# A delta rule with a routed expert layer: later index stores for the middle router run, and 816 rows an expert

## The chip, the core and the metric

The kernel runs on one core of a Trainium2 chip. A core has a matrix engine (TensorE, PE in the profile; its weight loads are shown as PEld), a vector engine (VectorE, DVE), a scalar engine (ScalarE, ACT), a general engine (GpSimd, POOL) and an engine that issues transfers (SyncE, SP). Each takes its own instructions in order, and they wait for one another by semaphores. Transfers run on 16 DMA engines; SP, ACT and POOL issue them. The metric is the time of one execution on the device in microseconds (us).

## The reference, cut to what matters

Two blocks follow one another. The first is a delta rule: for 4 batches and 8 heads of width 48 a state of 48 x 48 is carried over 768 steps.

```python
for t in range(S):
    y[:, :, t] = np.einsum('bhd,bhde->bhe', q[:, :, t], state)
    v_old = np.einsum('bhde,bhd->bhe', state, kt)
    state = state + bt[:, :, :, None] * np.einsum('bhd,bhe->bhde', kt, vt - v_old)
```

Its 3072 tokens of width 384 are then routed to the two best of eight experts by noisy logits, and each expert is a layer of 384 to 1024 to 384:

```python
noisy_logits = x @ w_gate + np.log1p(np.exp(x @ w_noise)) * noise
top2 = np.argpartition(-noisy_logits, 2, axis=1)[:, :2]
# top2_w: the two logits' softmax
for e in range(E):
    for k in range(2):
        mask = top2[:, k] == e
        h = np.maximum(x[mask] @ w1[e], 0.0)
        out[mask] += top2_w[mask, k, None] * (h @ w2[e])
```

## The kernel before

**Two stages.** `deltanet` (from L463) computes the delta rule, the routing and a first part of expert 0; after it, a loop over experts 1 to 7 does the rest. All is in 32-bit floating point.

**The delta rule.** The 768 steps are cut into 12 chunks of 64; two chunks make a step `s`, of which there are NS = 6, with US = 4 units each (a unit is one chunk of two batches). A unit ends in `answer`: a last product on PE (L1012), a copy by ACT to a buffer `y` of a ring of four (L1038), a store of it to memory by SP (L399, `rows_y`), three transposes on PE (L1022) and the product with the router's weights (L1027).

**The router.** `route(g)` runs three times, by `ROUTES = [(0, 3), (3, 2), (5, 1)]`: for steps 0 to 2, for steps 3 and 4 (the middle run), and for step 5. DVE finds for each token its two experts, and the row that the token gets in each expert's list: the `slot`s (the last of them are written at L1157). Then POOL stores for each unit, once for each of the two choices, a record (token, weight, place) at those rows of `tokens_x` in memory, with an indirect DMA of 128 records (L441, `spread`). These are the index stores: 24 for the first run, 16 for the middle one, 8 for the last.

**The early part of expert 0.** After step 2 and after step 4 (`EARLY`) enough of expert 0's tokens are known to start on them. `early_rows(s)` has SP read the table of the first records (`early_meta`, L1282) and POOL gather the rows that it names (`early_x`, L405): two blocks of 128 rows in the first group, three in the second. `early(s, lo, hi)` then transposes them on PE (L1326), multiplies by w1 (L1347, results rectified by ACT at L1358) and by w2 (L1371), in three batches: blocks 0 and 1, blocks 2 and 3, block 4.

**What sets the order.** Inside `deltanet` nothing is issued directly. Each piece is added to a list (`jobs.add`) with its engine, an estimated cost, the names that it reads and writes, and perhaps a due time (`due`), a spacing (`apart`), or a latest class (`late`). `Jobs.order` carries the due times backwards along the dependences and then walks forward through an estimated time, taking on each engine the most urgent job that could start. The result is the order in which each engine's instructions are issued; SP and POOL, which issue transfers, are ordered in the same way. What an instruction waits for on the chip is decided separately, from the buffers that it really touches and from the dependences that are added by hand: a name in `reads` alone places a job in the order, and makes no semaphore.

A name in the list `looked_up` of `route` makes a run's stores come behind the reads of the early tables of earlier steps. In POOL's queue the end of the delta rule stands thus, behind the last scaling of v (L917): the last of the first run's stores, two gathers of the first early group, the sixteen stores of the middle run, the three gathers of the second group, the eight stores of the last run. SP has, at the same place, the first table read, the stores of the last two `y`, the second table read (which waits for all stores of steps 0 to 4) and the loads of expert 1's weights.

**The experts.** An expert takes ROWS = TILES * 128 + MORE rows = 832 of its list. Should one have more tokens, a fallback after the loop (`tc.If(count > ROWS)`) does the remaining ones. `load_metas` reads the lists (L425, after every index store), `load_rows` gathers six blocks of 128 rows and one of MORE into `xr` (L405), `regroup` moves them by DMA into `xq` (L1609), and `turns` transposes these on DVE into `xe` (L1619). The first product is a fast scheme with 20 block products instead of 24, in which an operand has half the rows, RH = ROWS / 2 = 416 columns (`first`, by `PLAN`; all of its matmuls are issued at L1595, and its sums of operands at L1561). ACT copies and rectifies (L1651, L1662), DVE adds (L1656). The second product (`second`, also L1595, 192 columns) and the last rows (`last_rows`, L1706: MORE rows, in two halves of the array side by side) follow, and POOL adds the gated rows to the output (L460). `rest` does for expert 0 the 192 rows that the early part left (L1735 to L1768), while POOL and DVE prepare expert 1.

The lines of the hand-over are these; the rest stands below.

```python
turn_r = turn_of[s][0]
if s + 1 == sum(ROUTES[turn_r]):
    route(turn_r)
if s in EARLY:
    cut(s, EARLY[s][-1][1] * 128)
    early_rows(s)
```

Of the kernel before, what the change touches and what calls it, by code (L numbers as in the profile page):

```python
# [21 lines left out]
Q = 32  # L22
QS = 128 // Q
TILES = 6
MORE = 64
# [212 lines left out]
def kernel(  # L238
# [231 lines left out]
    def deltanet(ictx):  # L470
# [611 lines left out]
        def route(g):  # L1082
# [141 lines left out]
            for x in range(units):  # L1224
                of, i = first_s + x // US, x % US
                for y, to in enumerate(slot):
                    jobs.add(
                        POOL, 1.3,
                        lambda x=x, of=of, y=y, to=to: [
                            spread(metas(g)[:, x, y], to[:, x : x + 1], of, columns)  # L1230
                        ],
                        reads=[("slot", g % 2), meta, ("num", g % 2), "blank", *looked_up],
                        writes=[("rows", of, i, y)], lands=2.0, moves=0.2,
                        due=FIRST + (s + paced) * PACE + BEHIND + jobs.AFTER,
                        apart=jobs.APART * paced,
                    )

# [36 lines left out]
        def early_rows(s):  # L1274
# [6 lines left out]
            def load_meta():  # L1281
# [9 lines left out]
                SP, 0.7, load_meta, reads=of_steps, lands=2.0, moves=0.3, due=FIRST + s * PACE + BEHIND,  # L1291
# [3 lines left out]
            for at in range(lo, upto):  # L1295
                x, x_key = early_x[at], ("early_x", at)
                jobs.add(
                    POOL, 1.2,
                    lambda x=x, at=at: [take_rows(x, place_of(early_meta[:, at]), units)],
                    reads=[("early_meta", lo), *(("stored", i) for i in range(units))],  # L1300
                    writes=[x_key], lands=2.0, moves=0.7, due=FIRST + s * PACE + BEHIND,
                )
# [130 lines left out]
        for s in range(NS):  # L1433
# [37 lines left out]
            turn_r = turn_of[s][0]  # L1471
            if s + 1 == sum(ROUTES[turn_r]):
                route(turn_r)
            if s in EARLY:
                cut(s, EARLY[s][-1][1] * 128)
                early_rows(s)
# [26 lines left out]
    with ExitStack() as ectx:  # L1503
# [96 lines left out]
        def load_rows(e):  # L1600
            for i, size in enumerate(rows_in):
                take_rows(xr[0:size, i], place_of(metas_x[0:size, e, i]), NT)
# [13 lines left out]
        def turns():  # L1616
# [4 lines left out]
            some = TILES // 2  # L1621
            for i in range(2):
# [7 lines left out]
            more = MORE // Q  # L1630
            yield turn(
                xe[:, :, MAIN : MAIN + MORE].rearrange("p k (g x) -> p k g x", g=more),
                xq[:, 0:more, TILES].rearrange("p g (j k) -> p k g j", k=KT),
            )
# [295 lines left out]
```

## Time and profile before

| what | value |
|---|---|
| timed runs | 813.46, 810.22, 808.51 us; median 810.22 |
| the profiled execution | 825.89 us |
| its span, first to last instruction | 824.1 us |
| PE busy | 718.1 us, 87% of the span |
| PEld busy | 561.7 us |
| DVE busy | 541.7 us |
| POOL busy | 417.7 us |
| ACT busy | 307.8 us |
| mean granted clock of PE | 0.887 |
| DMA traffic | 79.60 MB |

The profile is one execution taken by the hardware profiler. Its page gives for each engine the busy time and its course in 40 slices of about 20.6 us (a digit is tenths of the slice), the clock that PE was granted in tenths of full speed (PEclk), groups of instructions by source line with their number and mean time, and what ended the idle time before them. Answers of the trace list the instructions of one engine in order of time (start, length, engine, line, operation, tiles out<-in, shape, number, and in brackets the idle time before with its cause), or the busy time of all engines in given stretches. "issue" stands for idle time for which the profile shows no cause. Ends of matmuls are modelled, so their starts are the safer marks.

The delta rule takes the first 323 us or so, the early part of expert 0 goes from there to 383 us, `rest` to 401 us, and the experts 1 to 7 take 58.6 us each.

### The profile page before, as it was taken

How to read it: one execution, taken by the hardware profiler on the slowest of the kernel's cores; microseconds unless marked ns; L12 is line 12 of the kernel's file. 1: busy time of each engine (PE TensorE's matmuls, PEld its weight loads, DVE VectorE, ACT ScalarE, POOL GpSimd, SP SyncE). 2: the span in 40 equal slices, each digit the busy share in tenths (PEclk: the TensorE clock that was granted, in tenths of full speed). 3: DMA queues.
4: the chain of work that ended last, by engine and by line, in shares of the span. 5: the costliest groups of instructions: out<-in, count | busy, mean ns of one | idle time of the engine just before them, and what ended most of it. 6: DMA issues, size and time to landing. Idle time of an engine off the chain costs nothing.

```text
span 824.1 us, 22389 instructions
## 1 busy us (share of the span) xinstructions
PE 718.1 (87%) x9319; PEld 561.7 (68%) x9319; DVE 541.7 (66%) x1100; ACT 307.8 (37%) x728; POOL 417.7 (51%) x408
## 2 busy tenths in 40 slices
PE   5656888887788862999999999999999999999993
PEld 3445777776677752778568668678588597596693
DVE  7899969898762420303488488587686785785831
ACT  3758486856445421122250340430520511502500
POOL 5030021021133445459678777786886886787032
PEclk8556788888677685999999999999999999999997
DMA  3457544322434011335644535544544446333031
GB/s 68 88 103 179 139 127 105 81 61 62 127 71 119 3 52 59 134 84 85 181 114 117 124 102 121 136 132 72 151 145 93 107 138 130 89 58 41 2 39 24
DMA packets 142719, 79.60 MB, mean 97 GB/s; under 512 B 118352, under 2 KB 139024, under 8 KB 141584
## 3 DMA queue, kind: packets, MB, share of 16 engines
q1 hardware_dynamic: 125840, 57.25, 26.8%
q0 software_dynamic: 12800, 19.80, 13.3%
q8 instruction: 75, 1.23, 0.7%
q10 hardware_dynamic: 3968, 1.03, 0.6%
q14 instruction: 36, 0.29, 0.1%
HBM read 49.85 MB, written 20.03 MB: 85 GB/s over the span
## 4 chain that ended last, share of the span: by engine, by line
PE 62%; DVE 14%; issue 12%; POOL 4%; ACT 2%; SPq 2%; DMA 1%; another core or an unknown queue 0%; DVEq 0%; POOLq 0%
PE inner L1595 24%; PE outer L1595 12%; DVE w2e L766 4%; PE pair L1347 3%; PE pair L635 3%; PE pair L1371 3%; DVE w1e L770 2%; POOL out_dram L460 2%; PE single L1027 2%; PE pair L1012 2%; PE inner L1706 2%; PE pair L975 2%; PE single L619 2%; DVE w2e L770 1%; PE pair L953 1%
## 5 line engine op out<-in xcount | busy, mean ns | idle before, releaser
L1662 ACT ACTIVATE hT<-inner 128x416 f32<-128x416 f32 x112 | 57.9, 517 | 260.9 <-PE inner L1595 257.6
L1656 DVE TENSOR_TENSOR hT<-hT,inner 128x416 f32<-128x416 f32 x182 | 105.5, 587 | 63.5 <-PE inner L1595 55.3
L460 POOL DMA_INDIRECT out_dram<-sums,metas_x x51 | 83.4, 1635 | 94.7 <-DVE sums L1495 67.3
L441 POOL DMA_INDIRECT tokens_x<-meta,slot x48 | 47.5, 989 | 79.6 <-DVE w2e L770 22.0
L1595 PE MATMUL inner<-s_x,w1e 128*128 128x416 f32 x196 | 78.7, 512 | 0.0
L917 POOL TENSOR_TENSOR v<-v,norms 128x384 f32<-128x384 f32 x24 | 23.7, 1008 | 91.1 <-DMA rows_y<-y 44.6
L405 POOL DMA_INDIRECT xr<-rows_y,metas_x x49 | 55.8, 1138 | 19.6 <-issue 12.8
L1651 ACT ACTIVATE hT<-hT 128x416 f32<-128x416 f32 x112 | 59.9, 547 | 12.1 <-DVE hT L1656 6.5
L1595 PEld LDWEIGHTS inner<-s_x,w1e 128*128 128x128 f32 x196 | 37.2, 190 | 31.2 <-issue 28.8
L1595 PE MATMUL inner<-xe,w1e 128*128 128x416 f32 x140 | 58.1, 513 | 0.0
L1595 PE MATMUL outer<-t_w,hT 128*128 128x192 f32 x336 | 58.0, 326 | 0.0
L1595 PE MATMUL inner<-s_x,s_w 128*128 128x416 f32 x140 | 56.9, 512 | 0.0
L1595 PEld LDWEIGHTS outer<-t_w,hT 128*128 128x128 f32 x336 | 55.2, 190 | 0.0
L1561 POOL TENSOR_TENSOR w1e<-w1e 128x256 f32<-128x256 f32 x63 | 52.8, 846 | 2.3
L1595 PE MATMUL outer<-w2e,hT 128*128 128x192 f32 x280 | 50.7, 328 | 0.3
L1595 PEld LDWEIGHTS outer<-w2e,hT 128*128 128x128 f32 x280 | 46.1, 190 | 4.3 <-issue 2.1
L1595 PEld LDWEIGHTS inner<-s_x,s_w 128*128 128x128 f32 x140 | 26.6, 190 | 22.3 <-issue 22.3
L824 ACT COPY w<-tt_tb 32x256 f32<-32x256 f32 x96 | 38.6, 402 | 6.8 <-DVE tt_tb L801 4.2
L1595 PE MATMUL outer<-t_w,s_h 128*128 128x192 f32 x224 | 40.6, 329 | 0.0
L1595 PEld LDWEIGHTS inner<-xe,w1e 128*128 128x128 f32 x140 | 26.4, 190 | 20.7 <-issue 16.5
L1491 DVE TENSOR_SCALAR sums<-outer,metas_x 128x192 f32<-128x192 f32 x70 | 27.8, 411 | 18.2 <-PE outer L1595 17.5
L1595 PEld LDWEIGHTS outer<-t_w,s_h 128*128 128x128 f32 x224 | 36.6, 190 | 4.2 <-issue 4.2
(202 smaller groups left out, 1586.7 us busy)
## 6 DMA issues: line engine op xcount, KB each, us to landing
w1e<-in_moe_w_dram SPq DMA_DIRECT2D x8, 1536.0 KB
w2e<-in_moe_w_dram SPq DMA_DIRECT2D x8, 1536.0 KB
v<-in_v_dram SPq DMA_DIRECT2D x48, 96.0 KB
qp<-in_q_dram SPq DMA_DIRECT2D x48, 96.0 KB
out_dram<-empty SPq DMA_DIRECT2D x4, 1152.0 KB
rows_y<-y SPq DMA_DIRECT2D x24, 192.0 KB
xq<-xr SPq DMA_DIRECT2D x52, 84.0 KB
kp<-in_k_dram SPq DMA_DIRECT2D x88, 48.0 KB
```

Of the source, the lines that this page charges most:

```text
L405: d = nc.gpsimd.indirect_dma_start(out=got, out_offset=None, in_=rows_y[0 : units * 128], in_offset=bass.IndirectOffsetOnAxis(ap=index, ax ...
L441: d = nc.gpsimd.indirect_dma_start(out=tokens_x, out_offset=bass.IndirectOffsetOnAxis(ap=slot, axis=0), in_=meta, in_offset=None, bounds_c ...
L460: d = nc.gpsimd.indirect_dma_start(out=out, out_offset=bass.IndirectOffsetOnAxis(ap=index, axis=0), in_=got, in_offset=None, bounds_check= ...
L635: nc.tensor.matmul(out[to(z, b), z, j], kT[rows_of[z], j, crossed(z, b)], rhs(z, j, b), start=(j == 0), stop=(j == NP - 1), skip_group_che ...
L766: v_.tensor_tensor(out=part, in0=t[:, :, j + 1 :, j, None].to_broadcast(shape), in1=t[:, :, None, j, 0:j].to_broadcast(shape), op=ALU.mult,)
L824: lambda rows=rows, cols=cols, w64=w64, tt=tt: nc.scalar.copy(w64[rows, :, cols], tt[rows]),
L1491: nc.vector.tensor_scalar_mul(got, p, gate)
L1561: engine.tensor_tensor(out=block(to), in0=block(x), in1=block(y), op=ALU.add if sign == "+" else ALU.subtract,)
L1595: nc.tensor.matmul(p, lhsT, rhs, start=opens and i == 0, stop=i == len(products) - 1, skip_group_check=True,)
L1651: nc.scalar.activation(h, h, ACTF.Relu)
L1656: nc.vector.tensor_tensor(out=h, in0=h, in1=p, op=ALU.add if sign > 0 else ALU.subtract)
L1662: nc.scalar.mul(h, p, float(sign))
```

## The change

There are three parts in the diff.

The index stores of the middle router run (`s + 2 == NS`, so steps 3 and 4) are no longer added to the list right after its slots. `route` now returns a function that adds them, `spread_all`; for the middle run it is held back and called after the last step's answers have been added. There the stores read one more name, the `y` of the last unit, their due time is one step later, and they lose their spacing. The other two runs call it at once, without that name.

The second early group's table read and gathers (`early_rows` for step 4) are added there too, behind those stores, and come due two steps later.

An expert takes 816 rows instead of 832: MORE is 48. The gather of the last block (`load_rows`), its regrouping and its transpose keep the depth of 64 rows, now named TAKEN. Since 64 rows of that transpose reach into the columns of the next part of `xe`, it moves from the end of `turns` to its start, and the later transposes overwrite the surplus. Everything that is made from ROWS, RH or MORE follows: 408 columns in the first product, 176 columns in `rest`, 48 rows in the last blocks.

```diff
@@ -22,7 +22,7 @@
 Q = 32
 QS = 128 // Q
 TILES = 6
-MORE = 64
+MORE, TAKEN = 48, 64
 EARLY_BANK = 2, (0, 1, 2)
 EARLY = {2: [(0, 2)], 4: [(2, 4), (4, 5)]}
 EARLY_TILES = 5
@@ -1221,7 +1221,13 @@
                 due=FIRST + s * PACE + BEHIND - SOONER[g],
             )
             jobs.add(DVE, 0.9, weights, reads=["r_p1"], writes=["r_den", meta])
-            for x in range(units):
+            slot_key = ("slot", g % 2)
+
+            def spread_all(lately):
+                for x in range(units):
+                    spread_of(x, lately)
+
+            def spread_of(x, lately):
                 of, i = first_s + x // US, x % US
                 for y, to in enumerate(slot):
                     jobs.add(
@@ -1229,11 +1235,13 @@
                         lambda x=x, of=of, y=y, to=to: [
                             spread(metas(g)[:, x, y], to[:, x : x + 1], of, columns)
                         ],
-                        reads=[("slot", g % 2), meta, ("num", g % 2), "blank", *looked_up],
+                        reads=[slot_key, meta, ("num", g % 2), "blank", *looked_up, *lately],
                         writes=[("rows", of, i, y)], lands=2.0, moves=0.2,
-                        due=FIRST + (s + paced) * PACE + BEHIND + jobs.AFTER,
-                        apart=jobs.APART * paced,
+                        due=FIRST + (s + (3 if lately else paced)) * PACE + BEHIND + jobs.AFTER,
+                        apart=jobs.APART * (paced and not lately),
                     )
+
+            return spread_all
 
         def cut(s, rows):
 
@@ -1288,7 +1296,7 @@
                         tc.add_manual_dep(d, w.name, SYNC, reason="tokens so far")
 
             jobs.add(
-                SP, 0.7, load_meta, reads=of_steps, lands=2.0, moves=0.3, due=FIRST + s * PACE + BEHIND,
+                SP, 0.7, load_meta, reads=of_steps, lands=2.0, moves=0.3, due=FIRST + (s + 2 * (s + 2 == NS)) * PACE + BEHIND,
                     writes=[("early_meta", i) for i in range(lo, upto)],
                 )
             units = (s + 1) * US
@@ -1298,7 +1306,7 @@
                     POOL, 1.2,
                     lambda x=x, at=at: [take_rows(x, place_of(early_meta[:, at]), units)],
                     reads=[("early_meta", lo), *(("stored", i) for i in range(units))],
-                    writes=[x_key], lands=2.0, moves=0.7, due=FIRST + s * PACE + BEHIND,
+                    writes=[x_key], lands=2.0, moves=0.7, due=FIRST + (s + 2 * (s + 2 == NS)) * PACE + BEHIND,
                 )
 
         def early(s, lo, hi):
@@ -1469,11 +1477,19 @@
             for n in units:
                 answer(n, recur(n))
             turn_r = turn_of[s][0]
+            if s + 1 == NS:
+                held["spread"]([("y", (NCH * NU - 1) % NY)])
+                early_rows(s - 1)
             if s + 1 == sum(ROUTES[turn_r]):
-                route(turn_r)
+                spread_all = route(turn_r)
+                if s + 2 == NS:
+                    held["spread"] = spread_all
+                else:
+                    spread_all([])
             if s in EARLY:
                 cut(s, EARLY[s][-1][1] * 128)
-                early_rows(s)
+                if s + 2 < NS:
+                    early_rows(s)
         for s, batches in EARLY.items():
             for lo, hi in batches:
                 early(s, lo, hi)
@@ -1599,7 +1615,8 @@
 
         def load_rows(e):
             for i, size in enumerate(rows_in):
-                take_rows(xr[0:size, i], place_of(metas_x[0:size, e, i]), NT)
+                n = TAKEN if i == TILES else size
+                take_rows(xr[0:n, i], place_of(metas_x[0:n, e, i]), NT)
 
         def regroup(queues=(nc.sync,)):
 
@@ -1618,7 +1635,11 @@
             def turn(out, in_):
                 return lambda: nc.vector.transpose(out=out, in_=in_)
 
-            some = TILES // 2
+            some, more = TILES // 2, TAKEN // Q
+            yield turn(
+                xe[:, :, MAIN : MAIN + TAKEN].rearrange("p k (g x) -> p k g x", g=more),
+                xq[:, 0:more, TILES].rearrange("p g (j k) -> p k g j", k=KT),
+            )
             for i in range(2):
                 for k in range(KT):
                     yield turn(
@@ -1627,11 +1648,6 @@
                             "p g i j -> p i g j"
                         ),
                     )
-            more = MORE // Q
-            yield turn(
-                xe[:, :, MAIN : MAIN + MORE].rearrange("p k (g x) -> p k g x", g=more),
-                xq[:, 0:more, TILES].rearrange("p g (j k) -> p k g j", k=KT),
-            )
 
         def first(a1, sums):
 
```

## The prediction

> **What bounds the kernel now.** I read the page first (busy rows, granted clock, cost groups), then the execution stretch by stretch, then PE and GpSimd around the hand-over from the delta rule to the experts.
>
> The page's head and its PE and clock rows:
> ```profile
> span 824.1 us, 22389 instructions
> PE   5656888887788862999999999999999999999993
> PEclk8556788888677685999999999999999999999997
> ```
> From the seventeenth slice (about 330 us) PE is full at full clock to the end; the two slices before are the emptiest of the run. Two of the stretches:
> ```profile
> 310.00:320.00 10.00, 0.00 (x0) 0.00 (x0) 0.00 (x0) 0.00 (x0) 7.86 (x8) 0.50 0.02 1
> 440.00:500.00 60.00, 59.96 (x276) 45.03 (x275) 44.54 (x80) 16.38 (x32) 46.69 (x42) 1.00 0.47 115
> ```
> The columns after the length are PE, PEld, DVE, ACT, POOL, then clock and DMA. From 330 us the experts are bound by PE alone: DVE and POOL have a quarter of each stretch left, so what PE saves or loses there is saved or lost at the end. The hole before it belongs to POOL, shown by its timeline:
> ```profile
> 321.58 0.98 POOL L441 DMA_INDIRECT tokens_x<-meta,slot  x1 [0.31 <-issue]
> 328.71 1.04 POOL L405 DMA_INDIRECT early_x<-rows_y,early_meta  x1 [6.14 <-DMA early_meta<-tokens_x]
> 330.06 1.02 POOL L405 DMA_INDIRECT early_x<-rows_y,early_meta  x1 [0.31 <-issue]
> 331.38 1.00 POOL L405 DMA_INDIRECT early_x<-rows_y,early_meta  x1 [0.30 <-issue]
> 341.27 1.02 POOL L441 DMA_INDIRECT tokens_x<-meta,slot  x1 [8.89 <-issue]
> ```
> L441 at 321.58 is the last of the middle router's sixteen stores. Then come the three gathers of the second early group, then, at 341.27, the first of the last router's eight, which waited for DVE's slots (written at 340.84). POOL stood free for 8.89 us between. PE at that time:
> ```profile
> 339.45 10.57 PE L1371 MATMUL pair<-w2e,tt_tb 128*128 128x384 f32 x32
> 349.85 1.55 PE L1326 MATMUL pair<-ident,early_x 128*128 128x128 f32 x9
> 351.30 10.63 PE L1347 MATMUL pair<-early_xe,w1e 128*128 128x256 f32 x48
> ```
> PE transposes the three gathered blocks at 349.85 without a wait: they were issued 18 us before.
>
> **Where the profiled execution stands.** It took 825.89 us (span 824.1 and 1.8 around it), 15.7 above the median of 810.22 and above all three runs. In it PE stood still from 306.94 to 322.96, put down to "issue", with ACT's last answer behind it. A hole of that size hardly fits into runs that are 15.7 us shorter, so I cost the change with it and without it.
>
> **What of the change reaches the engines.** Comparing the two built programs engine by engine, up to the experts PE, ACT, DVE and SP have the same instructions in the same order. The new read of the last answer is one of the planner only; no semaphore comes of it, and the sixteen middle stores stay where they were, behind the last scaling of v and the first two gathers. One thing moves: on POOL the last router's eight stores now stand ahead of the three gathers. SP's read of their table (L1282) keeps its place. Among the instructions of the experts, 416 columns become 408, 192 become 176, and the last tile's turn comes first. Loads and regrouping stay 64 rows deep.
>
> **Rows, a gain.** The groups of L1595 with 128x416 count 196+140+140+84 = 560. In PE's timeline 76 of them start between 402.45 and 428.99: 349 ns each, 0.839 ns a column. Eight columns fewer save 6.7 ns, times 560 = 3.8 us. L1746 has 48 of 192 columns, 162 ns apart; 16 columns less is 0.65 us. L1706's narrower blocks still stream 384 columns in pairs on both halves of the array: no gain. Sum **-4.4 us**. Between -3 (where an eviction sets the pace inside a stage it shrinks less; ACT's 517 ns and DVE's 587 hold a fixed part) and -4.5. The moved turn is one of seven on DVE, which has 15 us of each 60 free, and its extra waits on DVE itself lie in that room; uncovered they would cost well under 1 us per expert. The largest expert of these inputs has 807 tokens, below 816, so the fallback behind the expert loop stays unused.
>
> **The order on POOL, a loss.** Eight stores from 341.27 to 351.33 at a pitch of 1.29 us cannot come sooner here: their slots come from DVE at 341.01. The gathers follow at 351.63, 352.98 and 354.30 by their own pitch (1.35 and 1.32). How long one takes to land: the seventh xr gather is issued at 365.13 and SP, waiting for it, goes on at 368.47, 3.3 us. So the third block is there at 357.6. PE is in order; behind its L1371 block, ending about 350, stand these transposes and nothing else. A third of the 1.55 us after the landing, and ACT's copies beside it, put the start of L1347 at 358.3 instead of 351.30: **+7.0 us**. Low end 6.7 (landing in 3.05, as the trace marks the first xr gather). High end 9.9: before, the three gathers landed 6.1 to 6.6 us after issue by the trace's landing marks (335.3 to 337.5), while the weights of expert 1 were arriving. I take 3.3, since from 345 to 355 DMA is busy 0.02 of the time, as it is for xr and not as it was at 330.
>
> Who waits behind: POOL's xr gathers (357.25 before) start when the table read after the last store is in, which does not move; the three gathers end at 355.3, inside the 5.92 us that POOL idled there. The rest of PE's queue slides with L1347: ACT issues its half of the regrouping behind L1358, DVE's turns and sums follow and were done at 395.7 against a first use at 400.95, and they slide by the same amount. PE's later holes (0.66 and 0.41 us at 383 to 385) belong to copies that slide too, so nothing gives it back.
>
> Without the hole of 16 us: the slots come at about 323, but the last router's stores also read the early table (the list looked_up), which landed at 327.8; they start at 328.7 and end at 338.8. Gathers at 339.1 to 341.7, landed by 345.0, L1347 at 345.7. Before, the gathers landed at 337.5 and L1347 would start at 338.1. The cost is 7.6 us: nearly the same in either execution.
>
> **The clock, a loss beside it.** In the before-trace it fell within 3 us of PE's stop and came back late. The first three columns are again the stretch and PE; the clock is the third number from the end:
> ```profile
> 302.00:303.00 1.00, 0.00 (x0) 0.00 (x0) 0.00 (x0) 0.00 (x0) 0.79 (x1) 0.91 0.69 201
> 329.00:330.00 1.00, 1.00 (x4) 0.77 (x3) 0.02 (x1) 0.00 (x0) 0.75 (x1) 0.50 1.02 418
> 330.00:331.00 1.00, 1.00 (x6) 0.90 (x5) 0.29 (x2) 0.50 (x2) 0.94 (x1) 0.94 0.95 393
> ```
> And PE's timeline there:
> ```profile
> 327.20 12.05 PE L1347 MATMUL pair<-early_xe,w1e 128*128 128x256 f32 x48
> ```
> PE is busy again from 327.20, the clock returns at 330.13, and these 48 products take 12.05 us against 10.63 for the same 48 at 351.30: 1.4 us lost. The Trainium skill (TensorE: Matmul & The Clock Gate, "The HAM clock gate") says that one idle window of about 3.4 us halves the clock and that a busy window of 3.4 us must pass before it returns, with windows that run free. The new hole of some 5 us from 350 to the first landing contains or straddles such a window, so the rule speaks against this change; by it the restart costs 0.9 to 2.6 us, by the row 1.4. No loss at all is possible when two windows share the hole, or where an execution without the 16 us hole already paid for a cold clock before. I take the row, **+1.4**, and 0 to 3 as ends.
>
> **Sum.** -4.4 + 7.0 + 1.4 = +4.0 us: 829.9 profiled, **814.2** for the median. Half a per cent.
>
> **The rivals.**
> *The gathers are covered and only the rows count.* -4.4 gives 805.8. For it: most of the before's 18 us of lead was unused, and timed runs may reach the transposes later than the trace. Against it: stores and slots keep their distance to PE's L1371, 10.57 us, while eight stores and a landing need 17. Chance 0.17.
> *The stall is longer, slower by over 1%.* One mechanism: the gathers stand behind a queue of stores still being carried out, so they take the 6.1 us that they took before, and PE stays cold for a second window. 9.9 + 3.0 - 4.4 = +8.5, or 818.7. It decides from landings of about 6 us. For it: the three rows nearest in kind took that long. Against it: the weights explain those. Chance 0.19.
> *The middle stores really disturb the delta rule's end, and moving them lifts it.* The 16 us hole coincides with their burst (302.21 to 322.56). If half of it were also in timed runs and went: -8 - 4.4 gives 797.8. Against it: the burst isn't moved at all, and the eight stores from 341 to 351 disturb nothing. That the change doesn't do what its words say is thus what I expect of the middle stores. Chance 0.06.
> The forecast itself has 0.58.
>
> **How the numbers follow.** About 1% (8.1 us) is what a measurement of this kernel can tell from no change; the three runs spread over 5 us. Faster by over 1%: the third rival and a little for unforeseen order effects, 0.08. Slower by over 1%: the second rival, 0.19. Within: 0.73. The range takes in the first rival below and the second above, 804.5 to 819. The likeliest case alone, with the ends of landing and clock, is 811 to 818.
>
> **What the changed profile would show.** L1595 inner at 128x408, starts about 342 ns apart, an expert's period 58.6 going to 58.0 us. POOL: twenty-four L441 and then three L405 of early_x. PE: L1326 waits for DMA of early_x for about 5 us, in three pieces, L1347 of 256 columns starts some 17 us after the first of the last eight stores, at half clock. DVE and POOL as before in the expert stretches. I am wrong if PE reaches L1326 without waiting, if L1347 follows those stores by over 20 us, if the 408 columns leave gaps on PE between L1595 groups, or if the end of the delta rule itself shifts.

## The result, and the profile after

The kernel after took 818.69 us (median; 816.49 to 821.38) against 809.48 for the one before on the same chip: ratio 1.0101, 95% interval 1.0062 to 1.0139. The forecast was 814.2: the sign is right, the size is half. The profiled execution of after took 819.74 us, close to its median, so its trace can be read as it is.

First the head of the page of after, its PE row and its granted clock:

```profile
span 818.0 us, 22418 instructions
PE   5656888889878889398999999999999999999993
PEclk8556788795786789699999999999999999999997
```

The emptiest slice is the seventeenth (327 to 347 us), where before it was the sixteenth (the fifteenth, at 6, is no emptier than the first slices, against what the prediction reads there); the clock has its last low digit before the end there too. The two stretches shown of before, now of after (columns: length, PE, PEld, DVE, ACT, POOL, clock, DMA share, GB/s):

```profile
310.00:320.00 10.00, 10.00 (x47) 8.37 (x46) 4.05 (x25) 2.78 (x8) 7.56 (x9) 1.00 0.04 3
440.00:500.00 60.00, 59.88 (x279) 45.40 (x278) 44.08 (x80) 16.17 (x32) 46.47 (x41) 1.00 0.47 115
```

PE was idle from 310 to 320 in the profile of before and is full here, although POOL's burst of middle stores runs beside it as it did there. The stop of 16 us is absent. The experts are bound by PE as before. POOL's timeline of after:

```profile
319.80 0.98 POOL L441 DMA_INDIRECT tokens_x<-meta,slot  x1 [0.30 <-issue]
326.02 0.98 POOL L441 DMA_INDIRECT tokens_x<-meta,slot  x1 [5.24 <-DMA early_meta<-tokens_x]
...
336.33 1.04 POOL L405 DMA_INDIRECT early_x<-rows_y,early_meta  x1 [0.30 <-issue]
337.68 1.02 POOL L405 DMA_INDIRECT early_x<-rows_y,early_meta  x1 [0.31 <-issue]
339.00 1.00 POOL L405 DMA_INDIRECT early_x<-rows_y,early_meta  x1 [0.31 <-issue]
```

L441 at 319.80 is the last of the sixteen middle stores, which are where they were. The eight last stores wait for the early table, follow at 1.29 us each, and only then come the three gathers. PE of after in the same time and on to the first product of the experts:

```profile
318.07 10.57 PE L1379 MATMUL pair<-w2e,tt_tb 128*128 128x384 f32 x32
342.07 0.91 PE L1334 MATMUL pair<-ident,early_x 128*128 128x128 f32 x3 [13.43 <-DMA early_x<-rows_y,early_meta]
...
344.59 12.02 PE L1355 MATMUL pair<-early_xe,w1e 128*128 128x256 f32 x48
356.44 10.48 PE L1379 MATMUL pair<-w2e,tt_tb 128*128 128x384 f32 x32
...
378.23 1.10 PE L1751 MATMUL outer<-ident,rest_x 128*128 128x128 f32 x6 [0.66 <-DVE counts L1549]
381.29 6.42 PE L1762 MATMUL inner<-xe_r,w1e 128*128 128x176 f32 x30 [1.96 <-ACT xe_r L1755]
...
398.20 1.64 PE L1611 MATMUL inner<-xe,w1e 128*128 128x408 f32 x4
```

PE is through with L1379 at 328.64 and waits 13.43 us for the first gathered block. A second wait, 1.96 us for the copy `xe_r`, was not in the forecast, and the group behind it takes 6.42 us for narrower products than the 5.14 of before. The clock says why; from the stretches of after, it is the third number from the end:

```profile
333.00:334.00 1.00, 0.00 (x0) 0.00 (x0) 0.00 (x0) 0.00 (x0) 0.69 (x2) 0.89 0.33 95
347.00:348.00 1.00, 1.00 (x5) 0.85 (x4) 0.00 (x0) 0.38 (x1) 0.70 (x2) 0.78 0.39 141
382.00:383.00 1.00, 1.00 (x6) 1.00 (x5) 0.00 (x0) 0.00 (x0) 0.00 (x0) 0.50 1.12 160
385.00:386.00 1.00, 1.00 (x8) 1.00 (x8) 1.00 (x3) 0.34 (x2) 0.00 (x0) 1.00 0.69 15
```

It is halved from 333.8 to 347.4, as forecast for the wait, and a second time from about 381.6 to 385.0.

**How the profiles are compared.** The delta rule ends at another time in each execution, so I cut the execution at two marks of PE into three stretches: A, from the end of the first L1371 block of the early part (L1379 in after) to the start of the second 256-column L1347 block (L1355), which is the wait for the second early group; B, from there to the first product of the experts (L1595, L1611 in after); C, from there to the end of the span. For after: A = 344.59 - 328.64 = 15.95, B = 398.20 - 344.59 = 53.61, C = 818.0 - 398.20 = 419.8. The same three, for the executions told of below:

| kernel, run | order on POOL | rows | A | B | C |
|---|---|---|---|---|---|
| before, first profile | before | 832 | 1.29 | 49.65 | 423.20 |
| before again, e1 | before | 832 | 1.28 | 49.65 | 423.45 |
| before a third time, e9 | before | 832 | 7.69 | 51.51 | 422.95 |
| rows alone, e2 | before | 816 | 1.29 | 48.95 | 419.48 |
| rows alone, e6 | before | 816 | 7.94 | 50.49 | 419.80 |
| rows alone, e11 | before | 816 | 8.64 | 50.34 | 419.45 |
| order alone, e3 | after | 832 | 8.64 | 56.19 | 423.13 |
| after, first profile | after | 816 | 15.95 | 53.61 | 419.79 |
| after again, e5 | after | 816 | 15.73 | 53.37 | 420.01 |
| after, regrouping by SP, e7 | after | 816 | 15.92 | 50.50 | 419.60 |
| rows alone without the middle stores, e8 | before | 816 | 1.30 | 48.95 | 417.78 |
| the same again, e10 | before | 816 | 1.29 | 50.63 | 417.84 |
| rows alone, earlier first table, e12 | before | 816 | 1.29 | 48.95 | 419.86 |

(The values are from unrounded times. The profiled execution of e6, 814.27 us, is the slowest of its runs.) The rows are C and 0.7 us of B. The order is A and the rest of B. A has two levels for each order, and which one an execution has hangs on PE's stop at the end of the delta rule: with it PE comes so late that the gathers have a lead.

### The profile page after: what moved, and what is told of

Same layout as the page of the kernel before. It is cut to its first block, busy times and chain, and to the rows that moved or that the text cites. A ratio compares the mean times of both kernels' runs of the same rounds, so it can differ in the third digit from the quotient of the medians.

```text
span 818.0 us, 22418 instructions
## 1 busy us (share of the span) xinstructions
PE 718.5 (88%) x9319; PEld 565.6 (69%) x9319; DVE 540.5 (66%) x1100; ACT 307.0 (38%) x728; POOL 415.2 (51%) x408
## 4 chain that ended last, share of the span: by engine, by line
PE 53%; issue 16%; DVE 14%; POOL 8%; DMA 4%; SPq 2%; ACT 1%; POOLq 0%; DVEq 0%; ACTq 0%
PE inner L1611 25%; PE outer L1611 12%; PE pair L635 3%; DVE w2e L766 3%; POOL tokens_x L441 3%; POOL out_dram L460 2%; PE inner L1722 2%; DVE s_x L1577 2%; DVE w2e L770 2%; DVE w1e L770 1%; PE single L1027 1%; PE pair L975 1%; DMA tokens_x<-meta,slot 1%; PE pair L908 1%; PE pair L953 1%
## 5 line engine op out<-in xcount | busy, mean ns | idle before, releaser
L1678 ACT ACTIVATE hT<-inner 128x408 f32<-128x408 f32 x112 | 57.2, 511 | 259.4 <-PE inner L1611 258.0
L1672 DVE TENSOR_TENSOR hT<-hT,inner 128x408 f32<-128x408 f32 x182 | 104.1, 579 | 61.2 <-PE inner L1611 54.0
L460 POOL DMA_INDIRECT out_dram<-sums,metas_x x51 | 82.6, 1619 | 105.2 <-DVE sums L1511 67.7
L441 POOL DMA_INDIRECT tokens_x<-meta,slot x48 | 47.4, 987 | 71.5 <-DVE w2e L770 21.5
L1611 PE MATMUL inner<-s_x,w1e 128*128 128x408 f32 x196 | 77.4, 506 | 0.0
L1667 ACT ACTIVATE hT<-hT 128x408 f32<-128x408 f32 x112 | 59.1, 540 | 11.7 <-DVE hT L1672 6.3
L1611 PE MATMUL outer<-t_w,hT 128*128 128x192 f32 x336 | 58.0, 326 | 0.0
L1611 PEld LDWEIGHTS inner<-s_x,w1e 128*128 128x128 f32 x196 | 37.2, 190 | 29.9 <-issue 28.5
L1611 PE MATMUL inner<-xe,w1e 128*128 128x408 f32 x140 | 57.2, 507 | 0.0
L1611 PE MATMUL inner<-s_x,s_w 128*128 128x408 f32 x140 | 56.0, 506 | 0.0
L1611 PEld LDWEIGHTS outer<-t_w,hT 128*128 128x128 f32 x336 | 55.2, 190 | 0.0
L1577 POOL TENSOR_TENSOR w1e<-w1e 128x256 f32<-128x256 f32 x63 | 53.5, 858 | 2.4
L1611 PE MATMUL outer<-w2e,hT 128*128 128x192 f32 x280 | 50.7, 328 | 0.7
L1611 PEld LDWEIGHTS outer<-w2e,hT 128*128 128x128 f32 x280 | 46.1, 190 | 4.6 <-DVE sums L1507 2.5
L1611 PEld LDWEIGHTS inner<-s_x,s_w 128*128 128x128 f32 x140 | 26.6, 190 | 21.4 <-issue 21.4
L1611 PE MATMUL outer<-t_w,s_h 128*128 128x192 f32 x224 | 40.6, 329 | 0.0
L1611 PEld LDWEIGHTS inner<-xe,w1e 128*128 128x128 f32 x140 | 26.4, 190 | 19.8 <-issue 15.6
L1391 DVE TENSOR_SCALAR early_x<-pair,early_meta 128x384 f32<-128x384 f32 x5 | 3.1, 618 | 55.3 <-PE pair L1379 55.3
```

What stands on the lines that cost most here:

```text
L441: d = nc.gpsimd.indirect_dma_start(out=tokens_x, out_offset=bass.IndirectOffsetOnAxis(ap=slot, axis=0), in_=meta, in_offset=None, bounds_c ...
L460: d = nc.gpsimd.indirect_dma_start(out=out, out_offset=bass.IndirectOffsetOnAxis(ap=index, axis=0), in_=got, in_offset=None, bounds_check= ...
L1577: engine.tensor_tensor(out=block(to), in0=block(x), in1=block(y), op=ALU.add if sign == "+" else ALU.subtract,)
L1611: nc.tensor.matmul(p, lhsT, rhs, start=opens and i == 0, stop=i == len(products) - 1, skip_group_check=True,)
L1667: nc.scalar.activation(h, h, ACTF.Relu)
L1672: nc.vector.tensor_tensor(out=h, in0=h, in1=p, op=ALU.add if sign > 0 else ALU.subtract)
```

## The experiments

Each kernel was timed beside the one before on the same chip, and each ratio is against that. The chips differ: for e1 to e4 (one chip) and e12 (another) the kernel before had a median of 826 and 828 us, for e5 to e8 and e9 to e11 (two more) one of 811 and 812. In every profile taken on the first two, PE stands still for 11 to 21 us in all beside the burst of the sixteen middle stores, and for less than 3 us in those taken on the others. The first profile of before has the stop; by their medians (810 and 809 us) the timed runs of before that stand with it and with after most likely do not. The chip of that profile is not on record.

### The kernel before again (e1, e9)

No edit. For e1:

> The kernel before, unchanged, profiled a second time. Theory (the 16 us stop of PE at 306.9 to 323.0 in the profile of before is a feature of that one execution): this profile has no stop of PE of over 5 us between 295 and 320, the first 256-column block L1347 starts at 303 to 306, the second at 335 to 339, right behind the landing of the second early group, and the execution takes 806 to 813 us. Rival (the stop belongs to the kernel before, and the change takes it away): the stop is there again, the execution takes 820 to 828 us.

Measured: 826.16 us, and the stop is there again, as it is in the other three profiles from that chip (e2 to e4): there it belongs to the kernel before, as the rival has it, but also to the order of after (e3, e4), which therefore does not take it away. For e9:

> The kernel before a third time, for a profile of it without PE's stop at the end of the delta rule (both profiles of it so far have the stop, the six others without it are of other kernels). Theory (without the stop PE waits for the second gathers already before the change, as in e6: L1326 waits some 5.6 us, 7.9 us from the end of the first L1371 block to the second L1347 block, which runs at half clock at first): 7.5 to 8.5 us there, 51.2 us from L1347 to the first L1595 (49.65 with a warm clock), 806 to 813 us. Rival (the wait of e6 came of its disturbed execution): 1.3 us and 49.65. Where the stop is there again, 1.3 us and 820 to 828 us.

Measured: 814.00 us and no stop. PE of before in e9:

```profile
319.54 10.57 PE L1371 MATMUL pair<-w2e,tt_tb 128*128 128x384 f32 x32
334.96 0.91 PE L1326 MATMUL pair<-ident,early_x 128*128 128x128 f32 x3 [4.86 <-DMA early_x<-rows_y,early_meta]
...
337.80 12.49 PE L1347 MATMUL pair<-early_xe,w1e 128*128 128x256 f32 x48
350.12 10.48 PE L1371 MATMUL pair<-w2e,tt_tb 128*128 128x384 f32 x32
...
371.91 1.10 PE L1735 MATMUL outer<-ident,rest_x 128*128 128x128 f32 x6 [0.66 <-DVE counts L1533]
373.42 5.14 PE L1746 MATMUL inner<-xe_r,w1e 128*128 128x192 f32 x30 [0.41 <-ACT xe_r L1739]
```

This is the profile that belongs to the runs of 809 to 813 us: before the change, too, PE waits 4.86 us for the second group, and its second L1347 block is partly at half clock (12.32 us to the next block, against 10.47 in e1). So the kernel before already paid for a wait and a cold restart, and the change makes the wait longer.

### The rows alone (e2, e6, e11)

Against before; the turns of the last tile and its 64 loaded rows as in after:

```diff
-MORE = 64
+MORE, TAKEN = 48, 64
...
-                take_rows(xr[0:size, i], place_of(metas_x[0:size, e, i]), NT)
+                n = TAKEN if i == TILES else size
+                take_rows(xr[0:n, i], place_of(metas_x[0:n, e, i]), NT)
```

> Only the rows: 816 per expert and 64 taken, with the order of before (three gathers ahead of the last eight stores). Theory (rows gain 4.4 us, the order costs all the rest): 805 us, ratio 0.9946, L1595 of 408 columns 342 ns apart. Rival (the 816 rows bring their own cost at the start of the experts, where the profile of after has a second half-speed window at 381 to 385 and PE waiting 1.96 us for the copy of the rest rows, so the rows are worth only about 1 to 2 us): 808 us, ratio 0.998, with that window and that wait also here.

> The rows alone once more, since e2 left them between -4.4 and +2.0 us while its trace shows -0.7 us from L1347 to the first L1595 and -3.7 to -4.0 us from there to the end. Theory (the rows gain 4.4 us and e2 was noise of the part ahead of the experts): ratio 0.9946. Rival (something ahead of the experts gets slower with them): ratio 0.998 to 1.000.

> The rows alone a third time, since e2 and e6 lie apart (0.9985 and 0.9919). Theory (the traces' segments, -0.7 and -3.4 to -4.0 us, are all of it): 0.9946, interval some 0.003 wide to each side. Rival (816 rows also shorten something ahead of the experts): 0.992.

Measured: e2 0.9985 (0.9947 to 1.0024), e6 0.9919 (0.9891 to 0.9947), e11 0.9943 (0.9919 to 0.9966). By the times e2 fits its rival, e6 lies below what its theory gave, and the interval of e11 holds both its theory (0.9946) and its rival (0.992); by the traces all three are alike. C falls from 423.2 to 419.6 and B by 0.70 (e1 to e2), without the second cold window and with 0.37 us of wait before L1746. What e2's time lacks to that lies most likely in the part with the stop, on whose chip the kernel before itself runs from 818 to 833 us. e11 has the narrowest interval: -4.6 us. The rows are worth what was forecast, and this kernel, 808.19 us beside 812.46, beats both: it is the change without its order.

### The order alone (e3)

Against before:

```diff
+            if s + 1 == NS:
+                held["spread"]([("y", (NCH * NU - 1) % NY)])
+                early_rows(s - 1)
...
-                early_rows(s)
+                if s + 2 < NS:
+                    early_rows(s)
```

with the due times of the middle stores, of the table read and of the gathers as in after.

> Only the order: last eight stores ahead of the three gathers, rows as before (832, 416 columns). Theory (the order costs all of what is missing, 9.2 + 4.4 = 13.6 us): 823 us, ratio 1.0168. Rival (the order costs the 8.4 us of the prediction and the rows gain nothing): 818 us, ratio 1.0104.

Measured: 1.0173 (1.0116 to 1.0231), +14.3 us, the theory; the rival's 1.0104 lies outside. PE of e3:

```profile
362.35 2.55 PE L1334 MATMUL pair<-ident,early_x 128*128 128x128 f32 x9 [6.30 <-DMA early_x<-rows_y,early_meta]
364.69 10.35 PE L1355 MATMUL pair<-early_xe,w1e 128*128 128x256 f32 x42
...
378.43 10.59 PE L1379 MATMUL pair<-w2e,tt_tb 128*128 128x384 f32 x32 [1.41 <-ACT tt_tb L1366]
...
403.31 6.82 PE L1762 MATMUL inner<-xe_r,w1e 128*128 128x192 f32 x30 [1.88 <-ACT xe_r L1755]
```

A is 8.64, 7.36 more than in e1 (forecast for this case: 7.0). B is 6.5 more: 3.3 from L1355 to L1379 (1.4 of clock, 1.8 of waits for ACT), 1.5 of waiting at L1762, and 1.7 because that group runs cold. The last two are in after as well; the waits for ACT inside L1355 are not, and what brings them is not shown.

### After again (e5)

> The kernel after, unchanged, once more beside before on one chip. Theory (e2 and e3 add up: the rows take 4.4 us in the trace, the order costs 13.9 us, of which 7.4 us are PE's wait for the second gathers and 6.5 us come after it): ratio 1.0115, and between the start of the second 256-column block L1355 and the first L1611 53.6 us as in the profile of after, against 48.95 with the rows alone. Rival (the first comparison was a lucky pair of executions and the change is nearly free): ratio 1.000 to 1.004.

Measured: 817.44 us against 811.35, ratio 1.0085 (1.0056 to 1.0115): +6.9 us; the interval just reaches the theory's 1.0115 and leaves out the rival. A and B repeat. On this same chip the rows alone (e6) took 805.88, so the order costs 11.6 us by the medians; the traces give 7.8 in A and 2.9 in B. The line that A rests on, first of e5, then of e6:

```profile
337.09 2.46 PE L1334 MATMUL pair<-ident,early_x 128*128 128x128 f32 x9 [13.34 <-DMA early_x<-rows_y,early_meta]
```

```profile
338.42 0.91 PE L1326 MATMUL pair<-ident,early_x 128*128 128x128 f32 x3 [4.13 <-DMA early_x<-rows_y,early_meta]
```

### All regrouping by SP (e7)

Where does the wait for `xe_r` come from? The timelines of SP, ACT and POOL, first of after, then of before (e9):

```profile
341.21 0.98 SPq L425 DMA_DIRECT2D metas_x<-tokens_x  x2
344.90 1.00 POOL L405 DMA_INDIRECT xr<-rows_y,metas_x  x1 [4.90 <-PE pair L1334]
...
372.02 1.63 POOL L460 DMA_INDIRECT out_dram<-early_x,early_meta  x1 [0.16 <-issue]
372.69 7.77 ACTq L1626 DMA_DIRECT2D xq<-xr  x8
...
380.58 0.66 ACT L1755 COPY xe_r<-outer 128x384 f32<-128x384 f32 x2 [7.92 <-DMA out_dram<-early_x,early_meta]
```

```profile
345.96 0.99 SPq L425 DMA_DIRECT2D metas_x<-tokens_x  x2
349.20 1.04 POOL L405 DMA_INDIRECT xr<-rows_y,metas_x  x1 [6.83 <-PE pair L1347]
...
366.37 5.31 ACTq L1609 DMA_DIRECT2D xq<-xr  x8
372.56 0.81 ACT L1739 COPY xe_r<-outer 128x384 f32<-128x384 f32 x2 [6.23 <-PE outer L1735]
...
376.40 1.63 POOL L460 DMA_INDIRECT out_dram<-early_x,early_meta  x1
```

In e9 ACT is through with its eight transfers before POOL's five adds to the output (L460) begin. In after ACT, which comes behind PE, is 6.3 us later and POOL 4.4 us earlier (7.8 and 2.9 when both are counted from the end of the first L1371 block), so the adds fall on the transfers; ACT is done with its issues after 7.77 us instead of 5.31, and the copy stands behind them.

A single issue is not slower: its median is 629 ns in after and 619 in e9. The difference is three holes, before the fifth, sixth and seventh issue. The eight transfers use four semaphores in turn, and each hole ends when the earlier transfer on the same semaphore is in: the counts of the first three are full at 375.76, 377.05 and 379.18, and the issues start at 375.79, 377.07 and 379.20. These transfers took 3.1, 3.6 and 5.1 us from issue to landing; in e9 the first four took 2.1 to 2.3, and nothing waits. In all three profiles in which adds and transfers overlap (after, e3, e5) ACT needs 7.25 to 7.77 us, in the ten in which they do not 5.30 or 5.31. The bracket of the copy in after names the adds; in e7, below, the copy goes at 376.61 while adds are issued until 378.51, so it does not itself wait for them. The edit against after takes ACT out of that:

```diff
-            regroup([nc.sync, nc.scalar])
+            regroup([nc.sync])
```

> After, with all sixteen regrouping DMAs xq<-xr issued by SP instead of eight by SP and eight by ACT. Theory (PE slid by the wait, GpSimd did not: its five early adds to the output, L460, at 372 to 381 now fall on ACT's eight regrouping DMAs, whose issue takes 7.77 us instead of 5.30; the copy of the rest rows stands behind them on ACT, PE waits 1.96 us and loses a clock window): L1762 follows L1751 by 1.5 us instead of 3.06 and runs at full clock, 48.95 + 1.4 = 50.3 us from L1355 to the first L1611 instead of 53.6, ratio 3.3 us below e5, 1.0075. Rival (the copy waits for something else, or SP's sixteen issues come too late for DVE's turns): 53 us or more, ratio as e5 or above.

Measured: 1.0064 (1.0040 to 1.0088), 1.7 us less than e5 by the ratios, their intervals overlapping. The trace decides; PE of e7:

```profile
342.11 12.18 PE L1355 MATMUL pair<-early_xe,w1e 128*128 128x256 f32 x48
...
375.91 1.09 PE L1751 MATMUL outer<-ident,rest_x 128*128 128x128 f32 x6 [0.66 <-DVE counts L1549]
377.37 4.74 PE L1762 MATMUL inner<-xe_r,w1e 128*128 128x176 f32 x30 [0.37 <-ACT xe_r L1755]
...
392.60 1.64 PE L1611 MATMUL inner<-xe,w1e 128*128 128x408 f32 x4
```

L1762 follows L1751 by 1.46 us, at full clock, and B is 50.50, the 50.3 expected and that of the rows alone. The adds are still at 369 to 378. So the wait comes from ACT's transfers beside POOL's adds. Of the 2.9 us between e5 and e7 it is 1.1, and the cold window at L1762 1.7 (1.6 and 1.7 in after). That the window belongs to the wait is likely, but not shown: all three profiles with the wait have it, and of the eleven without it two have it too, e10 and e4:

```profile
363.77 6.42 PE L1746 MATMUL inner<-xe_r,w1e 128*128 128x176 f32 x30 [0.37 <-ACT xe_r L1739]
```

```profile
398.03 6.42 PE L1763 MATMUL inner<-xe_r,w1e 128*128 128x176 f32 x30 [0.37 <-ACT xe_r L1756]
```

### The weights of expert 1 later (e4)

Against after; the load is put behind the regrouping on SP:

```diff
-        w_even_tiles, weights = weights, load_weights(w_odd, 1)
+        w_even_tiles, weights = weights, w_odd
...
             regroup([nc.sync, nc.scalar])
+            load_weights(w_odd, 1)
```

> After, with the load of expert 1's weights (2 x 1.5 MB, issued by SP at 323.6 and moving until 334) put behind the regrouping DMAs on SP, so that nothing but stores and gathers moves from 323 to 345. Theory (the weights hold up the last stores, which landed up to 8 us after issue, and the gathers queue behind them): the gathers land about 3.3 us after issue instead of 4.5 to 5.7, L1355 starts about 17 us after the first of the last stores instead of 18.6, and the time falls by 1.4 to 3 us against after: 816 us, ratio 1.008. Rival (the queue of stores drains at its own pace, or the gathers have that latency whenever they follow stores): landings stay at 4.5 to 5.7 and the time at 818.7, ratio 1.011. If GpSimd's sums of the late weights come too late for the first L1611, it is slower than after.

Measured: 1.0324 (1.0264 to 1.0384): far slower, the third case of its expectation. On SP the load stands behind the regrouping and went out at 395.91 only, together with the last of ACT's eight transfers (issued from 391.03, behind ACT's share of PE's work; SP's own eight were out by 376.3). What held SP in between the trace does not say plainly. POOL's sums began when the load was in:

```profile
402.47 1.40 POOL L1577 TENSOR_TENSOR w1e<-w1e 128x256 f32<-128x256 f32 x2 [31.10 <-DMA w1e<-in_moe_w_dram]
```

The question it was made for has an answer all the same. The first gather was issued at 353.47 and PE used it at 358.26, 4.8 us later, with no weights moving; in e3, where they had been in since 341, it was 4.75 (357.60 to 362.35). In after, with the weights just in, 5.7 (336.33 to 342.07), in e5 5.7 and in e7 6.4. In the order of before, without the stop, it is 5.8 (e6) to 6.65 (e11). So a first gather of this group is used later than the 3.3 us of the forecast with the weights or without, and in both orders; that the stores ahead of it are the reason is not shown.

The run also tells the adds from the other suspects. In the order of after, but with the adds only from 421.86 on, ACT is done with its transfers in the usual time, and L1763 (L1762 of after) waits 0.37 us:

```profile
391.03 5.30 ACTq L1626 DMA_DIRECT2D xq<-xr  x8
```

### The middle stores left out (e8, e10)

Against the rows alone:

```diff
                         lambda x=x, of=of, y=y, to=to: [
                             spread(metas(g)[:, x, y], to[:, x : x + 1], of, columns)
-                        ],
+                        ] if g != 1 else [],
```

> Rows alone, order of before, with the middle router's sixteen stores L441 left out (their table rows stay blank, so that later gathers and adds address fewer tokens): everything that does not wait for them keeps its place. Theory (where PE and ACT stand still for up to 16 us at the end of the delta rule, it is the stores' burst on GpSimd's queue that holds them): no stop of PE of over 2 us between 295 and the first L1347, which starts at 303 to 306, and none inside it; the second group's gathers come some 20 us sooner and PE reaches L1326 without waiting: 8 to 20 us below e6, ratio 0.97 to 0.985. Rival (the stop has another cause): PE still stands still by over 5 us there, and the time falls by less than 8 us.

> Rows alone with the middle router's sixteen stores left out, once more, beside e9 on one chip, in case e9 shows PE's stop. Theory (the stores' burst is the cause of the stop): no stop of over 2 us at the end of the delta rule, even where e9 has it; 797 to 802 us. Rival (another cause): the stop is in both.

Measured: e8 0.9832 (0.9801 to 0.9862), 797.81 us, 8.1 below e6; e10 800.48. Both fell on chips where the other kernels show no stop, so of its cause they say nothing. Of the wait they do. PE of e8:

```profile
323.98 10.57 PE L1371 MATMUL pair<-w2e,tt_tb 128*128 128x384 f32 x32
334.38 1.54 PE L1326 MATMUL pair<-ident,early_x 128*128 128x128 f32 x9
335.84 10.63 PE L1347 MATMUL pair<-early_xe,w1e 128*128 128x256 f32 x48
```

The gathers go out at 310 and PE reaches L1326 without a wait: A is 1.30, B 48.95, together 8.2 us less than in e6 (C is 2.0 less, too; what brings that is not shown). The wait of the kernel before is thus set by the chain of sixteen stores, table read and gathers, to which the change adds eight stores.

### An earlier first table (e12)

Against the rows alone; the first run's last two stores no longer wait for DVE's progress:

```diff
-                            spread(metas(g)[:, x, y], to[:, x : x + 1], of, columns)
+                            spread(
+                                metas(g)[:, x, y], to[:, x : x + 1], of,
+                                [] if (g, x) == (0, units - 1) else columns,
+                            )
```

> Rows alone in the order of before, and the first router's last two stores no longer wait for DVE's progress (in e9 they stand 6.38 and 1.55 us idle for it, at 290.26 and 292.79, while the table read, the first gathers, the sixteen middle stores and the second gathers queue behind them). Theory (PE's wait for the second gathers is set by this chain, as the leaving out of the sixteen stores showed with -8 us): the whole chain comes about 6.5 us sooner, the stretch from the first L1371 block's end to the second L1347 block shrinks from 7.7-8.6 to 1.3-2 us and that block runs at full clock: 6 to 8 us below the rows alone, ratio 0.985 to 0.988. Rival (the stores' burst, now from 295 on beside the last steps of the delta rule, holds up PE and ACT there, which is what the pacing was for): the delta rule's end and the first L1347 shift late by as much, ratio 0.994 or above.

Measured: 1.0009 (0.9987 to 1.0031), which is the rival's case, on a chip with the stop, so A is 1.29 whatever the chain does. B and C are those of the rows alone; what the rows gained is lost ahead of A, where the first L1371 block ends at 355.09 against 349.35 in e2. Those are two chips, so that the earlier burst is the reason is not shown. And the chain gained less than meant: the two stores went at 284.51 and 285.79, but the table read came at 295.59, in SP's queue behind a store of an answer. The stop in PE's and ACT's timelines of e12:

```profile
318.49 1.10 PE L1012 MATMUL pair<-u,qk 64*64 64x48 f32 x30 [11.96 <-issue]
```

```profile
317.96 0.48 ACT L964 COPY u<-pair 128x384 f32<-128x384 f32 x1 [16.42 <-remote]
```

Whether an earlier chain pays where the stop is absent stays open.

## Why the forecast had the sign and half the size

**Rows, -4.4: right.** C falls from a mean of 423.2 (four profiles) to 419.7 (seven), 3.5 us where 3.8 were worked out for L1595, within its ends: the products start 342 ns apart, as forecast, and an expert takes 58.0 us instead of 58.5 (not the 58.6 given above). B falls by 0.70 where 0.65 was forecast. Together -4.2, and -4.6 in e11's time.

**What moves on POOL: right.** The last eight stores pass three gathers and nothing else; the middle stores and the delta rule's order stay. The end of the delta rule does not shift: the first L1371 block ends at 328.64, 323.75 and 326.18 in the order of after and at 330.11, 334.30 and 331.61 in that of before, but these executions were 1.1 above, 2.8 below, 1.5 below their kernels' medians, and 1.5, 8.4 and 3.6 above. If these differences lie ahead of the mark and are taken off, the means are 327.3 and 327.5.

**The stall, +7.0 with the stop and 7.6 without: right.** Measured 7.4 (e1 to e3) and 7.8 (mean A of the three without the stop in each order: 15.9 and 8.1). Inside the sum terms were off and nearly cancel. L1355 starts 5.6 us after the third gather's issue (339.00 to 344.59), not 4.0: the landing of 3.3 us was taken over from the later gathers, and the first of these takes 4.75 to 6.65 us to its use, in either order. The last stores began 6.2 us after the last middle store, not 7.1, and before the change L1347 started 0.5 us later behind that store than was put in. The first of these is the reading that the second rival spoke for. So 7.6 against 7.8 is in part luck; the chain of stores, gathers, PE is as forecast.

**The clock, +1.4: wrong here.** The forecast took the row of the profile with the stop; its own lower end, zero where the execution had already paid for a cold clock, was the case of the timed runs. From the second L1347 block to the next L1371 it is 12.32 us before (e9) and 11.85 after. In the case with the stop the term is there (1.4 in e3, within the 0.9 to 2.6 that the prediction estimates). What failed is the choice of the execution that the term was read from: it was 15.7 us above the median, and what it showed (a warm clock, gathers with 18 us of lead) was not so in the runs that count.

**Who waits behind: the step that failed.** The forecast had it that the table read on which POOL's later work hangs "does not move", and that the rest of PE's queue and ACT's transfers slide "by the same amount"; that the two could meet is not in it. But POOL does not slide with PE. Its first xr gather follows SP's table read by 3.0 to 4.8 us in all fourteen profiles, whatever the bracket names. With the stores ahead of the gathers that read goes at 341.21 instead of 345.96, the first xr gather at 344.90 instead of 349.20 and the adds at 372.02 instead of 376.40, while ACT comes 6.3 us later. Where the stop exists the read keeps its place, as forecast (some 4 us behind the end of the first L1371 block, in the first profile of before and in e3), but PE and ACT slide onto the adds there, too. This is +3.0 us in B (from 50.4 to 53.5): 1.1 to 1.6 of it the wait, which e7 shows to come from the meeting, and 1.7 the cold window that stood behind the wait each time.

**The sum.** -4.2 + 7.8 + 0 + 3.0 = +6.6 us, against +6.9 in e5 (4.5 to 9.3) and +8.2 by the first comparison's ratio (5.0 to 11.3). What may be left, up to 2 us there, lies within these intervals and has no place in the traces.

**The rivals.** The first (only the rows count) is excluded: e5 and e6 on one chip differ by 11.6 us. The second gave 818.7 and came nearest, by luck: of its mechanism the later landing is there, but before the change as well, so it adds nothing to the difference, and the second cold window is not at the stall; it begins 34 us after the first one has ended, behind the copy `xe_r`. The third (the middle stores' move lifts the end of the delta rule) does not hold: they are not moved, and where the stop exists it is in both orders (e1, e3).

## What to carry to other kernels

When a wait makes one engine later, list every engine that does not get later with it, and ask what the two now meet: here POOL ran ahead while PE and ACT slid, and two sets of transfers that used to follow one another fell together. Transfers issued by an engine that also computes can hold up its compute: ACT's copy stood behind issues that waited for their own earlier transfers. If the profiled execution lies well off the median, look for the part of the trace that cannot be in the timed runs and make the whole sum without it, the cover and the clock included. A change made of two edits is worth two kernels: the rows alone are worth 0.5%, and the order took away two and a half times as much.

## What the runs showed of the chip that was not expected

**The clock falls without a fully idle stretch.** In e5 PE waits 1.45 us at L1762, in after 1.96, and both then have one cold stretch of 3.4 us, which makes the group of thirty 176-column products 6.42 us instead of 4.74. In after PE was busy 1.4 of the 3.4 us ahead of the fall, in e5 2.0. In e10 and e4, with waits of only 0.66 and 0.37 us there, it was busy 2.4 of them, and the clock fell all the same:

```profile
360.88:364.29 3.41, 2.38 (x13) 1.78 (x13) 1.56 (x6) 0.71 (x2) 3.08 (x5) 1.00 0.65 89
365.00:366.00 1.00, 1.00 (x5) 1.00 (x4) 1.00 (x3) 0.32 (x1) 0.69 (x2) 0.50 1.36 50
```

These are two stretches of e10, with PE behind the length and the clock third from the end. The Trainium skill (TensorE: Matmul & The Clock Gate, "The HAM clock gate") asks for an idle window of about 3.4 us; the length of the cold stretch agrees with it, the condition does not: a stretch some 40 to 70% busy came ahead of the fall. What decides is not shown: with waits like those of e10 the clock held in nine profiles, in e8 over a stretch of 3.41 us (367.40 to 370.81) in which PE was busy 2.38 us as well.

**A stop that differs from chip to chip.** On two of the chips PE and ACT stand still for 11 to 21 us in all beside the sixteen stores, in both orders. In the longest of these stops the waiting instruction is one of ACT, for a semaphore count of PE's that comes 18 us after PE's products (in e3 they end at 311.42 and the count comes at 329.51):

```profile
329.53 0.48 ACT L1038 COPY y<-pair 128x384 f32<-128x384 f32 x1 [17.99 <-remote]
```

This is ACT of e3; PE's own line L1022 follows it at 330.06. The same burst, at the same pitch of 1.29 us, leaves PE alone on the other chips, also for the same kernels (before in e1 and e9; the rows alone in e2 and in e6 and e11), with one profile each. The stop was never seen apart from the burst, but the runs without the burst fell on chips without the stop, so its cause is open.
